# Fused state-space and gated-MLP kernel: later weight loads slot by slot over 128 partitions, and a reordered head

## The chip, the cores and the metric

One NeuronCore of a Trainium2 chip. The metric is the device time of one execution in microseconds; 182.97 is the median of three runs before the change (182.96 to 183.09). Beside it stands one profiled execution, which all views of the trace come from. PE is the matrix engine, DVE the vector engine, ACT the scalar engine, POOL the GpSimd engine, SP the engine whose queue issues most of the loads and stores.

## The reference

```python
def _A_ref(x, ...):                     # state space, P = D = 448 states
    Lam_bar = jnp.exp(dt * Lam)
    B_bar = ((Lam_bar - 1.0) / Lam)[:, None] * Bmat
    Bu = jnp.einsum("bld,pd->blp", x + 0j, B_bar)
    for t in range(L):                  # L = 2048 tokens
        h = Lam_bar[None, :] * h + Bu[:, t, :]
        hs.append(h)
    return 2.0 * jnp.einsum("blp,dp->bld", hseq, Cmat).real + x * Dskip

def _B_ref(x, w_gate, w_up, w_down):    # 448 -> 1792 -> 448
    g = jnp.einsum("bsd,df->bsf", x, w_gate)
    u = jnp.einsum("bsd,df->bsf", x, w_up)
    return jnp.einsum("bsf,fd->bsd", _sigmoid(g) * u, w_down)

xn = _layernorm(x)
out = x + _A_ref(xn, ...) * _silu(_B_ref(xn, ...))
```

All arrays are bfloat16: x is 1 x 2048 x 448, w_gate and w_up are 448 x 1792 each.

## The kernel before

The 2048 tokens are 16 tiles of 128 (x_all, loaded by load_x), taken in 4 chunks of 512. A chunk is normalized and transposed to xnT (feature rows in partitions, tokens along the free side). Its 448 feature rows are 7 slots of 64; xnT holds the slots twice, in partitions 0 to 63 and, rotated, in partitions 64 to 127, so that two matmuls of 64 rows run side by side. The weights wG and wU lie the same way: 7 slots of 64 rows; partitions 0 to 63 hold columns 0 to 895 of w_gate or w_up, partitions 64 to 127 columns 896 to 1791.

For each chunk PE runs 7 pairs of tiles of w_gate ("g" tiles m = 0 to 6) and of w_up ("u"); gu_mm (lines 805 to 809) gives each tile seven steps of two matmuls: step s takes slot s from partitions 0 to 63 and slot s+1 (mod 7) from 64 to 127. ACT takes the tanh of a g tile (gu_evac), DVE multiplies it into the u tile (hF, line 844). Then come the products with B (b_phase; bT and bT6 hold B transposed, bT3 its last rows), the scan on DVE, and in the following chunks the products with C (yout) and w_down (down), the gating and the stores.

Chunk 0 goes g0 to g6, u0 to u6, then b_phase; its head (lines 1099 to 1156) is written out by hand with one order for ACT and DVE (pl.seq): statistics of token tiles 0 to 3 (bn, aggr, root, recip, norm), PE transposes (split for tile 0, first_slots for tiles 1 to 3), copies out of PSUM (ACT, lines 578 and 592), copies within SBUF (DVE, line 599), and the 64-row matmuls of g0 and g1 for one token tile at a time (last_tile, line 814, with slots "a", "b", "c" or 1).

Every operation is given to a planner (class Plan) with a cost, the keys that it reads and writes, and for loads a landing time; solve lays them out and emit issues each engine's instructions in that order. The costs and landing times in the code decide only that order. Waits on the chip come from the data. Loads and stores on SP and ACT share eight completion semaphores in turn, so a load is issued only once the eighth before it has landed.

The loads that matter here: x tiles 0 to 3 and the first 256 columns of wG (load_w0, two queues), then on SP the rest of wG in four loads of 64 partitions (load_w), x tiles 4 and 5, wU's first block, x tiles 6 and 7, the rest of wU; then B by four DMA transposes (b_load), Dskip (dbc), the transposes of chunk 1, w_down (wd), C.

Of the kernel before, what the change touches and what calls it, by code (L numbers as in the profile page):

```python
# [14 lines left out]
ACT = mybir.ActivationFunctionType  # L15
# [3 lines left out]
D = 448  # L19
# [7 lines left out]
TPC = L // P  # L27
NTAB = L + 1
EPS = 1e-5
HEAD_DMA = 19  # L30
TWO_PI = 2.0 * math.pi
PI = math.pi
MAGIC = 12582912.0
# [213 lines left out]
def kernel(  # L247
# [118 lines left out]
    def load_w(eng, k, half, b, r=(), rate=105e3, land=0.0):  # L366
        m0, m1 = BLK[k][b]
        ps = slice(half * H, half * H + H)
        c0 = half * 896
        load(eng, [("w", k, half, m) for m in range(m0, m1)], H * 7 * (m1 - m0) * P * 2,  # L370
             wgt[k][ps, :, m0 * P:m1 * P],
             wsrc[k][:, c0 + m0 * P:c0 + m1 * P].rearrange("(s p) f -> p s f", p=H), cost=0.65, r=r, rate=rate, land=land)

    def load_w0(eng, half, part, r=(), land=0.0):
        ps = slice(half * H, half * H + H)
        s0, c0 = (1 - half if part == "A" else half), half * 896
        n = 4 - s0
        load(eng, [("w", "g", half, m, part) for m in range(2)], H * n * 2 * P * 2, wgt["g"][ps, s0:7:2, 0:2 * P],
             wsrc["g"][:, c0:c0 + 2 * P].rearrange("(s p) f -> p s f", p=H)[:, s0:7:2, :], cost=0.5, r=r, rate=400e3, land=land)

    def wkeys(k, m, part=None):
        if k == "u" or m > 1:
            return [("w", k, 0, m), ("w", k, 1, m)]
        if part == "b":
            return [("w", k, 0, m, "A"), ("w", k, 1, m, "A")]
        return [("w", k, h, m, q) for h in range(2) for q in "AB"]
# [14 lines left out]
    def load_p(eng, k, r=()):  # L401
# [13 lines left out]
    add("POOL", 0.15, lambda: G.memset(ident[:], 0.0), w=["ident"], chain=True)  # L415
    add("POOL", 0.4, lambda: G.affine_select(out=ident[:], in_=ident[:], compare_op=ALU.not_equal, fill=1.0, base=0,
                                             pattern=[[-1, P]], channel_multiplier=1), r=["ident"], w=["ident"], chain=True)
    load_w("SP", "g", 0, 1, rate=400e3, land=8.5)
    load_w("SP", "g", 1, 1, rate=400e3, land=9.5)
    load_w("SP", "g", 0, 2, rate=400e3, land=11.0)  # L420
    load_w("SP", "g", 1, 2, rate=400e3, land=12.4)
    load_x(4, 2, land=13.8)
    add("POOL", 0.1, lambda: G.memset(halfc[:], 0.5), w=["consts"])
    add("POOL", 0.1, lambda: G.memset(negc[:], -1.0), r=["consts"], w=["consts"])
    add("POOL", 0.1, lambda: G.memset(expc[:], math.e), w=["expc"])
# [3 lines left out]
                                    allow_small_or_imprecise_dtypes=True), w=[("wv", 0)])  # L429
    add("POOL", 0.15, lambda: G.memset(flat(g_raw[:, 512:2048], 3, 512)[:, :, D:512], 0.0),  # L430
        w=[("xnw", t) for t in (1, 2, 3)])
    load_w("SP", "u", 0, 0, rate=400e3, land=15.6)
    load_w("SP", "u", 1, 0, rate=400e3, land=16.8)
    load_x(6, 2, land=17.9)
    load_w("SP", "u", 0, 1, rate=400e3, land=19.0)
    load_w("SP", "u", 1, 1, rate=400e3, land=20.1)
    load_w("SP", "u", 0, 2, rate=400e3, land=21.6)
    load_w("SP", "u", 1, 2, rate=400e3, land=23.1)


    def warm_mm(n, w=512):
        def f():
            for _ in range(n):
# [14 lines left out]
    def stats(t):  # L458
        bn(t)
        aggr(t)  # L460
# [19 lines left out]
        ks = lambda k: [(k, t) for t in range(t0, t0 + n)]  # L480
        add("DVE", 0.08, lambda: V.reciprocal(out=rsd[:, t0:t0 + n, :], in_=sdb[:, t0:t0 + n, :]), r=ks("sd"), w=ks("rs"))

    def root(t):
        add("ACT", 0.2, lambda: A.activation(sdb[:, t, :], mvf[:, t, 1:2], ACT.Sqrt, bias=epsc[:]),
            r=[("mv", t), "sqrttab", "epsc"], w=[("sd", t)], lat=0.16)

    def act_mean(t):
        add("ACT", 0.62, lambda: A.activation(junk[:], x_all[:, t, :], ACT.Identity, scale=-1.0 / D, accum_out=nmf[:, t, :]),
# [122 lines left out]
    def xr(c, lo=0, hi=TPC):  # L611
        return [("xnT", c % 3, j, h) for j in range(lo, hi) for h in "ab"]
# [127 lines left out]
        add("POOL", 0.2, lambda: G.tensor_copy(out=sa7[H:P, :], in_=C("n2r")[H:P, 3:4]), r=["n2r"], w=["sa7b"])  # L740

    def b_load():
        for i, m in enumerate((A_B_re, A_B_im)):
            tload([("bT", i)], bT[:, 0:3, i, :], m[:, 0:384], D * 768, land=25.0 + 1.7 * i)
            tload([("bT3", i)], bT[:, 3:4, i, :], m[:, 320:448], D * 256, land=25.7 + 2.0 * i)
            add("POOL", 0.7, lambda i=i: G.tensor_copy(out=bT6[:, 0:3, i * H:i * H + H], in_=bT[:, 0:3, i, 384:448]),
                r=[("bT", i)], w=[("bT6", i)])
            if i == 0:
                add("POOL", 0.45, lambda: G.tensor_copy(out=bT[0:H, 3, 0, :], in_=bT[H:P, 3, 0, :]),
                    r=[("bT3", 0)], w=["bT3l"])  # L750
            for h in range(2):
                add("POOL", 0.25, lambda i=i, h=h: G.tensor_copy(out=bT6[h * H:h * H + H, 3, i * H:i * H + H],
                                                                        in_=bT[H:P, 3, i, 384:448]),
                    r=[("bT3", i)], w=[("bT6", i, h)])

    def c_load():
        for i, m in enumerate((A_C_re, A_C_im)):
# [56 lines left out]
    def last_tile(c, k, steps, j, hs="ba"):  # L814
        x, w_ = xnT[c % 3], wgt[k]
        ts = slice(j * P, j * P + P)
        for h in hs:
            ss = {"a": (0, 2, 4, 6), "b": (1, 3, 5), "c": (0, 2, 4), 1: (6,)}[h]
            for m, a in steps:
                ms = slice(m * P, m * P + P)  # L820

                def f(ms=ms, a=a, ss=ss):
                    for s in ss:
                        go, end = (s == 1, s == 6) if hs[0] == "b" or hs == "a" else (s == 0, s == 5)
                        T.matmul(gu[a][:, 0, ts], lhsT=w_[0:H, s, ms], rhs=x[0:H, SL[s], ts], start=go, stop=end)
# [44 lines left out]
    def b_phase(c, mid=None):  # L870
        x = xnT[c % 3]
        slots = [next_gu() for _ in range(3)]
        a3 = (next_acc(), next_acc())
        bk = [("bT", 0), ("bT", 1), ("bT3", 0), ("bT3", 1), "bT3l"]
        bk6 = [("bT6", 0), ("bT6", 1)] + [("bT6", i, h) for i in range(2) for h in range(2)]
        rs = [(slice(0, H), SL[6]), (slice(H, P), SL[5])]

        def halfrows(pt, start):
# [37 lines left out]
                        r=[("acc", a3[i])] + ([("bus", u, i, 0)] if h else []),  # L916
                        w=[("bus", u) if h == i == 0 else ("bus", u, i, h)])

        add("PE", 0.54, pairs, r=xr(c) + bk + bk6, w=key(3) + key(0) + key(1), name=f"bp{c}")
        for pt in (3, 0, 1):  # L920
            add("PE", (1.29 if pt < 3 else 0.66) + (SW if pt == 3 else 0), lambda pt=pt: fulls(pt, False),
                r=xr(c) + bk + bk6 + key(pt), w=key(pt), name=f"b{c}.{pt}")
# [3 lines left out]
        add("PE", 1.29, lambda: fulls(2, True), r=xr(c) + bk, w=key(2), name=f"b{c}.2")  # L926
        add("PE", 0.22 + SW, lambda: halfrows(2, False), r=xr(c) + bk + key(2), w=key(2), name=f"bp{c}.2")
        evac(2)

    bus_of = {}  # L930
# [127 lines left out]
    def yout(c, j, first=False):  # L1058
        t = c * TPC + j
        g, o, q = gt_of[c, j], next_o(), t % NXD  # L1060
        a = next_acc()
        key, ok, od = ("acc", a), ("o", o, 0), o_t[o][:]
        y = y_mm(c, j, acc[a], key, 0, D, False, first)
        add("DVE", dve1(D), lambda: V.tensor_tensor(out=od, in0=y, in1=xd[q][:], op=ALU.add), r=[key, ("xd", q)], w=[ok])
        add("DVE", dve2(D), lambda: V.tensor_tensor(out=od, in0=od, in1=g_t[g][:], op=ALU.mult), r=[ok, ("gt", g)], w=[ok])
        add("DVE", dve2(D), lambda: V.tensor_tensor(out=od, in0=od, in1=x_all[:, t, :], op=ALU.add), r=[ok, ("x", t)], w=[ok])
        rows = (0, H, P) if c == 2 and j == 3 else (0, P)
        for r0, r1 in zip(rows, rows[1:]):
            store(t, od, 0, D, r0, r1, [ok])

# [39 lines left out]
    aggr(2)  # L1110
    norm(0)
    act_root(1)
    stats(3)
    recip(1, 1)
    norm(1)

    def split(t, keys, banks, eng, between=None):
        pe_transpose(t, [(4, 7, keys[0], banks[0], eng[0]), (0, 4, keys[1], banks[1], eng[1])], between)
# [5 lines left out]
    def between_copies():  # L1124
        copies.append(columns(acc[1][:, 400:412], ("acc", 1)))
        last_tile(0, "g", steps01, 0, "b")
        root(2)
    split(0, ak, ab, ("ACT", "ACT"), between_copies)
    root(3)
    copies[0]()  # L1130
    add("NONE", 0.0, lambda: None, r=["pv0", ("xn", 1)], w=["pv"], lat=0.0)
    first_slots(1, uk[0], ub[0], "ACT")
    last_tile(0, "g", steps01, 0, "a")
    for t in (2, 3):
        recip(t, 1)
        norm(t)
        first_slots(t, ak[t - 2], ab[t - 2], "ACT")
    turns()
    for t in (1, 2, 3):
        shift(t, 1, "DVE")  # L1140
# [3 lines left out]
    scale(1)  # L1144
    silu_table()
    for t in (1, 2, 3):
        last_tile(0, "g", steps01, t, ("c", 1, "b"))
    gu_evac(0, "g", 0, slots0[0])
    gu_evac(0, "g", 1, slots0[1])
    scale(2)  # L1150
# [114 lines left out]
```

## Time and profile before

| | us |
|---|---|
| median of three runs | 182.97 |
| profiled execution, whole | 183.62 |
| its span (first to last instruction) | 181.8 |
| PE busy / DVE busy / ACT busy | 176.3 / 166.4 / 98.1 |
| first transposes on PE | 4.83 |
| g tile 2, first step on PE | 10.40 |
| u tile 0, first step on PE | 17.95 |
| first matmul with B | 28.53 |
| x tiles 4 and 5 read by DVE / tiles 6 and 7 | 13.76 / 18.76 |

Time on PE is dense when the starts follow each other at the pace of the matmuls; busy time alone does not say that, because matmuls overlap. In a timeline row the columns are start, duration, engine, line, operation, output and inputs, and in brackets the idle time before it and what ended it. A window row gives its stretch, the busy time and count of each engine, the granted PE clock, the mean busy share of the 16 DMA engines and GB/s. A queue's row gives its packets, MB and the time of its packets as a share of 16 engines' time.

### The profile page before, as it was taken

To read this page: it belongs to the slowest core of one execution; us is meant where nothing else is said; L and a number is where in the kernel's file an instruction comes from. 1 tells how busy PE (TensorE), PEld (TensorE's weight loads), DVE (VectorE), ACT (ScalarE), POOL (GpSimd) and SP (SyncE) were. 2 spreads that over 40 slices of the span, in tenths; PEclk is the share of its full clock that TensorE was granted. 3 is DMA by queue.
4 is the path that set the end of the run, shared out by engine and by line. 5 is a ranking of instruction groups with operands and counts; after the bars stand their busy time and mean duration, and the time that the engine had idled before them with its cause. 6 is when DMAs were issued, how large, how long until landed. Compare 5 with 4: busy or idle time off the path is not lost.

```text
span 181.8 us, 3610 instructions
## 1 busy us (share of the span) xinstructions
PE 176.3 (97%) x1404; PEld 88.0 (48%) x1411; DVE 166.4 (92%) x294; ACT 98.1 (54%) x162; POOL 37.2 (20%) x93
## 2 busy tenths in 40 slices
PE   8899998999999999999999999999999999999993
PEld 2764444564544444445554444444555444455552
DVE  3866889999989999999999999999999999999772
ACT  4999899958699985364145543348210533411101
POOL 6463556200008797000004100000000000000000
PEclk9999999999999999999999999999999999999999
DMA  5899989999200290000004900001000000002111
GB/s 129 234 216 217 171 159 183 258 251 226 72 0 0 50 140 15 0 4 0 0 2 82 134 14 0 4 0 62 14 4 0 25 27 26 3 0 76 58 54 48
DMA packets 30852, 13.43 MB, mean 74 GB/s; under 512 B 19441, under 2 KB 30834, under 8 KB 30834
## 3 DMA queue, kind: packets, MB, share of 16 engines
q1 hardware_dynamic: 30208, 12.83, 35.0%
q10 hardware_dynamic: 562, 0.36, 0.7%
q8 instruction: 11, 0.18, 0.4%
q14 instruction: 7, 0.06, 0.1%
q0 software_dynamic: 64, 0.00, 0.0%
HBM read 6.77 MB, written 1.84 MB: 47 GB/s over the span
## 4 chain that ended last, share of the span: by engine, by line
PE 81%; DMA 6%; DVE 4%; SPq 4%; ACT 2%; issue 1%; DVEq 0%
PE gu L807 34%; PE gu L1023 15%; PE acc L1042 11%; PE acc L1023 9%; PE gu L895 8%; DMA x_all<-in_A_x_dram 6%; SPq L357 4%; DVE hF L844 2%; PE acc L898 2%; PE gu L881 2%; ACT hT L680 1%; ACT xn L534 1%; DVE bst L450 1%; PE gu L808 1%; DVE spm L687 0%
## 5 line engine op out<-in xcount | busy, mean ns | idle before, releaser
L807 PE MATMUL gu<-xnT,wU 64*128 64x512 bf16 x196 | 45.8, 376 | 0.0
L808 PE MATMUL gu<-xnT,wU 64*128 64x512 bf16 x196 | 45.8, 376 | 0.0
L807 PE MATMUL gu<-xnT,wG 64*128 64x512 bf16 (+1 forms) x189 | 41.3, 360 | 0.0
L808 PE MATMUL gu<-xnT,wG 64*128 64x512 bf16 (+1 forms) x189 | 41.3, 360 | 0.0
L841 ACT ACTIVATE sig<-gu 128x1024 f32<-128x1024 f32 x21 | 21.3, 1019 | 24.7 <-PE gu L808 20.1
L1023 PEld LDWEIGHTS <-hF 128*128 128x128 bf16 x224 | 21.9, 98 | 20.6
L807 PEld LDWEIGHTS <-wU 64*128 64x128 bf16 x196 | 18.4, 94 | 22.9
L807 PEld LDWEIGHTS <-wG 64*128 64x128 bf16 x196 | 18.4, 94 | 19.9
L1023 PE MATMUL gu<-wd,hF 128*128 128x448 bf16 x140 | 28.0, 352 | 0.0
L844 DVE SCALAR_TENSOR_TENSOR hF<-sig,gu 128x1024 bf16<-128x1024 f32 x21 | 25.4, 1210 | 0.7 <-ACT sig L841 0.4
L1042 PE MATMUL acc<-cT,hT 128*128 128x448 bf16 (+2 forms) x119 | 22.9, 337 | 0.0
L962 DVE TENSOR_TENSOR_SCAN wv<-c_r,st,z 128x512 bf16<-128x512 f32 x18 | 22.8, 1273 | 0.0
L1029 ACT ACTIVATE g_t<-gu 128x448 bf16<-128x448 f32 x10 | 5.4, 540 | 27.7 <-PE gu L1023 16.8
L808 PEld LDWEIGHTS <-wU 64*128 64x128 bf16 x196 | 18.4, 94 | 0.0
L808 PEld LDWEIGHTS <-wG 64*128 64x128 bf16 x196 | 18.4, 94 | 0.0
L1023 PE MATMUL acc<-wd,hF 128*128 128x448 bf16 x84 | 16.9, 352 | 0.0
L1042 PEld LDWEIGHTS <-hT 128*128 128x128 bf16 x126 | 11.6, 98 | 9.9 <-issue 0.4
L895 PE MATMUL gu<-xnT,bT 128*128 128x512 bf16 x65 | 15.3, 379 | 0.4
L909 ACT CAST bus<-gu 128x1024 bf16<-128x1024 f32 x12 | 12.0, 1011 | 5.9 <-PE gu L881 5.3
L540 POOL COPY xn<-xn 128x448 bf16<-128x448 bf16 x12 | 7.5, 627 | 28.8 <-ACT xn L534 28.6
L450 DVE BATCH_NORM_STATS2 bst<-x_all 128x6 f32<-128x448 bf16 x11 | 6.4, 616 | 5.8 <-DMA x_all<-in_A_x_dram 5.8
L915 ACT CAST bus<-acc 64x256 bf16<-64x256 f32 (+1 forms) x24 | 8.7, 368 | 4.8 <-PE acc L898 4.4
(161 smaller groups left out, 264.1 us busy)
## 6 DMA issues: line engine op xcount, KB each, us to landing
wd<-in_B_w_down_dram SPq DMA_DIRECT2D x2, 784.0 KB, 6.4
out_dram<-o_t SPq DMA_DIRECT2D x14, 112.0 KB, 1.7
wU<-in_B_w_up_dram SPq DMA_DIRECT2D x4, 224.0 KB, 9.6
x_all<-in_A_x_dram SPq DMA_DIRECT2D x2, 448.0 KB, 5.0
wG<-in_B_w_gate_dram SPq DMA_DIRECT2D x2, 336.0 KB, 6.4
wU<-in_B_w_up_dram SPq DMA_DIRECT2D x2, 336.0 KB, 9.2
wG<-in_B_w_gate_dram SPq DMA_DIRECT2D x2, 224.0 KB, 4.8
x_all<-in_A_x_dram SPq DMA_DIRECT2D x2, 224.0 KB, 7.2
```

The costliest lines, as they stand in the source:

```text
L450: add("DVE", 0.56 if t < TPC else 0.6, lambda: V.bn_stats(out=bst[b][:], in_=x_all[:, t, :]), r=[("x", t)] + ([("xnT", 0, 3, "a")] if 3 < ...
L540: add("POOL", 0.25 if n == H else 0.6, lambda: G.tensor_copy(out=o[:, D:D + n], in_=o[:, 0:n]), r=[("xn", b)], w=[("xnw", b)])
L807: T.matmul(bank[0][:, ts], lhsT=w_[0:H, s, ms], rhs=x[0:H, SL[s], ts], start=(s == 0), stop=(s == 6))
L808: T.matmul(bank[1][:, ts], lhsT=w_[H:P, (s + 1) % 7, ms], rhs=x[H:P, SL[s], ts], start=(s == 0), stop=(s == 6))
L841: add("ACT", act(1024), lambda: A.activation(th, gu[a][:], ACT.Tanh, scale=0.5), r=[("gu", a)], w=[tk])
L844: add("DVE", dve1(1024), lambda: V.scalar_tensor_tensor(out=ho, in0=th, scalar=1.0, in1=gu[a][:], op0=ALU.add, op1=ALU.mult), r=[("gu", a) ...
L895: T.matmul(gu[slots[pt]][:, i, :], lhsT=bT[:, kt, i, pt * P:pt * P + P], rhs=x[:, kt, :], start=(first and kt == 0), stop=(not first and k ...
L909: add("ACT", act(1024), lambda: A.copy(out=bus[u][:], in_=gu[slots[pt]][:]), r=key(pt), w=[("bus", u)])
L915: add("ACT", 0.36, lambda ns=ns, d=d, q=q, l=l, i=i: A.copy(out=bus[u][d, l, ns], in_=acc[a3[i]][q, 0:256]), r=[("acc", a3[i])] + ([("bus" ...
L962: dve(1.194, lambda k=k: V.tensor_tensor_scan(out=wv[:, k, :], data0=rb, data1=z[:, k, :], initial=(st[pt][:, k, :] if c else 0.0), op0=AL ...
L1023: T.matmul(d, lhsT=hF[c % 2][:, m, h, js], rhs=wd[:, ft, :], start=(ft == 0), stop=(ft == FT - 1))
L1042: T.matmul(y, lhsT=hT[c % 2][:, hm, js], rhs=cT[:, cm, c0:c1], start=(i == 0 and not skip_on_pe), stop=(i == 6))
```

## The change

The later weights, that is wG from column 256 and all of wU, are loaded by load_rows: one load for each of the 7 slots, over all 128 partitions. x tiles 4 to 7 are loaded between wG and wU. Of token tile 0, slots 4 to 6 are copied out of PSUM by DVE instead of ACT; one root serves token tiles 2 and 3; the "c" matmuls of tiles 1, 2 and 3 come one tile earlier on PE than before. B's last rows are loaded before the rest of B, and b_phase's first matmuls name only those. The stores of chunk 2 and of chunk 1's last tile go in two halves. Only the first matmul into a bank of g0 and g1 now carries the start flag.

```diff
-HEAD_DMA = 19
+HEAD_DMA = 25
...
+    def load_rows(eng, k, s, m0, m1, land=0.0):
+        src = wsrc[k][s * H:s * H + H, :].rearrange("p (h f) -> h p f", h=2)[:, :, m0 * P:m1 * P]
+        load(eng, ("w", k, "s", s), P * (m1 - m0) * P * 2, wgt[k][:, s, m0 * P:m1 * P], src, cost=0.45, rate=400e3, land=land)
...
         if k == "u" or m > 1:
-            return [("w", k, 0, m), ("w", k, 1, m)]
+            return [("w", k, "s", s) for s in range(7)]
...
-    load_w("SP", "g", 0, 1, rate=400e3, land=8.5)
-    load_w("SP", "g", 1, 1, rate=400e3, land=9.5)
-    load_w("SP", "g", 0, 2, rate=400e3, land=11.0)
-    load_w("SP", "g", 1, 2, rate=400e3, land=12.4)
-    load_x(4, 2, land=13.8)
+    for s in range(7):
+        load_rows("SP", "g", s, 2, 7, land=7.7 + 0.5 * s)
+    load_x(4, 2, land=11.6)
+    load_x(6, 2, land=12.4)
+    for s in range(7):
+        load_rows("SP", "u", s, 0, 7, land=13.2 + 0.7 * s)
...
-    load_w("SP", "u", 0, 0, rate=400e3, land=15.6)
-    load_w("SP", "u", 1, 0, rate=400e3, land=16.8)
-    load_x(6, 2, land=17.9)
-    load_w("SP", "u", 0, 1, rate=400e3, land=19.0)
-    load_w("SP", "u", 1, 1, rate=400e3, land=20.1)
-    load_w("SP", "u", 0, 2, rate=400e3, land=21.6)
-    load_w("SP", "u", 1, 2, rate=400e3, land=23.1)
...
-    def root(t):
-        add("ACT", 0.2, lambda: A.activation(sdb[:, t, :], mvf[:, t, 1:2], ACT.Sqrt, bias=epsc[:]),
-            r=[("mv", t), "sqrttab", "epsc"], w=[("sd", t)], lat=0.16)
+    def root(t, n=1):
+        ts = range(t, t + n)
+        add("ACT", 0.2, lambda: A.activation(sdb[:, t:t + n, :], mvf[:, t:t + n, 1:2], ACT.Sqrt, bias=epsc[:]),
+            r=[("mv", q) for q in ts] + ["sqrttab", "epsc"], w=[("sd", q) for q in ts], lat=0.16)
...
     def b_load():
-        for i, m in enumerate((A_B_re, A_B_im)):
-            tload([("bT", i)], bT[:, 0:3, i, :], m[:, 0:384], D * 768, land=25.0 + 1.7 * i)
-            tload([("bT3", i)], bT[:, 3:4, i, :], m[:, 320:448], D * 256, land=25.7 + 2.0 * i)
...
+        src = (A_B_re, A_B_im)
+        for i in range(2):
+            tload([("bT3", i)], bT[:, 3:4, i, :], src[i][:, 320:448], D * 256, land=19.8 + 1.3 * i)
...
+        for i in range(2):
+            tload([("bT", i)], bT[:, 0:3, i, :], src[i][:, 0:384], D * 768, land=22.6 + 1.7 * i)
...
-                        go, end = (s == 1, s == 6) if hs[0] == "b" or hs == "a" else (s == 0, s == 5)
+                        go, end = (j == 0 and s == 1), (j == 3 and s == 5)
...
-        add("PE", 0.54, pairs, r=xr(c) + bk + bk6, w=key(3) + key(0) + key(1), name=f"bp{c}")
+        add("PE", 0.54, pairs, r=xr(c) + bh + bh6, w=key(3) + key(0) + key(1), name=f"bp{c}")
...
-        rows = (0, H, P) if c == 2 and j == 3 else (0, P)
+        rows = (0, H, P) if c == 2 or (c == 1 and j == 3) else (0, P)
...
-    stats(3)
-    recip(1, 1)
-    norm(1)
...
         last_tile(0, "g", steps01, 0, "b")
-        root(2)
-    split(0, ak, ab, ("ACT", "ACT"), between_copies)
-    root(3)
+        aggr(3)
+        root(2, 2)
+        recip(1, 1)
+        norm(1)
+    bn(3)
+    split(0, ak, ab, ("DVE", "ACT"), between_copies)
...
     last_tile(0, "g", steps01, 0, "a")
+    recip(2, 2)
     for t in (2, 3):
-        recip(t, 1)
         norm(t)
         first_slots(t, ak[t - 2], ab[t - 2], "ACT")
+        if t == 2:
+            last_tile(0, "g", steps01, 1, "c")
...
     for t in (1, 2, 3):
-        last_tile(0, "g", steps01, t, ("c", 1, "b"))
+        if t < 3:
+            last_tile(0, "g", steps01, t + 1, "c")
+        last_tile(0, "g", steps01, t, (1, "b"))
...
-    load("SP", "dbc", P * D * 2, dbc[:], A_Dskip.unsqueeze(0).to_broadcast((P, D)), rate=400e3, land=29.0)
+    load("SP", "dbc", P * D * 2, dbc[:], A_Dskip.unsqueeze(0).to_broadcast((P, D)), rate=400e3, land=26.5)
```

More of the change, by code (lines that the diff above doesn't have):

```diff
@@ L742, in b_load @@
     def b_load():
-        for i, m in enumerate((A_B_re, A_B_im)):
-            tload([("bT", i)], bT[:, 0:3, i, :], m[:, 0:384], D * 768, land=25.0 + 1.7 * i)
-            tload([("bT3", i)], bT[:, 3:4, i, :], m[:, 320:448], D * 256, land=25.7 + 2.0 * i)
-            add("POOL", 0.7, lambda i=i: G.tensor_copy(out=bT6[:, 0:3, i * H:i * H + H], in_=bT[:, 0:3, i, 384:448]),
-                r=[("bT", i)], w=[("bT6", i)])
+        src = (A_B_re, A_B_im)
+        for i in range(2):
+            tload([("bT3", i)], bT[:, 3:4, i, :], src[i][:, 320:448], D * 256, land=19.8 + 1.3 * i)
             if i == 0:
@@ L754, in b_load @@
                     r=[("bT3", i)], w=[("bT6", i, h)])
+        for i in range(2):
+            tload([("bT", i)], bT[:, 0:3, i, :], src[i][:, 0:384], D * 768, land=22.6 + 1.7 * i)
+            add("POOL", 0.7, lambda i=i: G.tensor_copy(out=bT6[:, 0:3, i * H:i * H + H], in_=bT[:, 0:3, i, 384:448]),
+                r=[("bT", i)], w=[("bT6", i)])
     def c_load():
@@ L873, in b_phase @@
         a3 = (next_acc(), next_acc())
-        bk = [("bT", 0), ("bT", 1), ("bT3", 0), ("bT3", 1), "bT3l"]
-        bk6 = [("bT6", 0), ("bT6", 1)] + [("bT6", i, h) for i in range(2) for h in range(2)]
+        bh = [("bT3", 0), ("bT3", 1), "bT3l"]
+        bh6 = [("bT6", i, h) for i in range(2) for h in range(2)]
+        bk = {pt: [("bT", 0), ("bT", 1)] if pt < 3 else [("bT6", 0), ("bT6", 1)] for pt in range(4)}
         rs = [(slice(0, H), SL[6]), (slice(H, P), SL[5])]
@@ L917, in evac @@
                         w=[("bus", u) if h == i == 0 else ("bus", u, i, h)])
-        add("PE", 0.54, pairs, r=xr(c) + bk + bk6, w=key(3) + key(0) + key(1), name=f"bp{c}")
+        add("PE", 0.54, pairs, r=xr(c) + bh + bh6, w=key(3) + key(0) + key(1), name=f"bp{c}")
         for pt in (3, 0, 1):
             add("PE", (1.29 if pt < 3 else 0.66) + (SW if pt == 3 else 0), lambda pt=pt: fulls(pt, False),
-                r=xr(c) + bk + bk6 + key(pt), w=key(pt), name=f"b{c}.{pt}")
+                r=xr(c) + bk[pt] + key(pt), w=key(pt), name=f"b{c}.{pt}")
             evac(pt)
@@ L925, in b_phase @@
             mid([None, *((("gu", a), gu[a][:, 0, 0:D]) for a in slots[:2]), None])
-        add("PE", 1.29, lambda: fulls(2, True), r=xr(c) + bk, w=key(2), name=f"b{c}.2")
-        add("PE", 0.22 + SW, lambda: halfrows(2, False), r=xr(c) + bk + key(2), w=key(2), name=f"bp{c}.2")
+        add("PE", 1.29, lambda: fulls(2, True), r=xr(c) + bk[2], w=key(2), name=f"b{c}.2")
+        add("PE", 0.22 + SW, lambda: halfrows(2, False), r=xr(c) + bh + key(2), w=key(2), name=f"bp{c}.2")
         evac(2)
```

## The prediction

> **What bounds the kernel now.** I read the page first, then the PE timeline, then the chain of waits, then the DMA by stretches.
>
> ```profile
> PE 176.3 (97%) x1404; PEld 88.0 (48%) x1411; DVE 166.4 (92%) x294; ACT 98.1 (54%) x162; POOL 37.2 (20%) x93
> PE 81%; DMA 6%; DVE 4%; SPq 4%; ACT 2%; issue 1%; DVEq 0%
> ```
>
> PE is the bound: 81% of the chain that ended last. The edits add and remove no matmul, so they can only change where PE waits. The timeline has two waits after the warm-up:
>
> ```profile
> 6.16 0.21 PE L825 MATMUL gu<-xnT,wG 64*128 64x128 bf16 x1 [0.48 <-ACT xnT L578]
> 29.32 0.39 PE L881 MATMUL gu<-xnT,bT 64*128 64x512 bf16 x2 [0.41 <-DVE hF L844]
> ```
>
> At 6.16 PE had waited for ACT's first copy out of PSUM. At 29.32 it waited for a bank that DVE freed late: the pair before started at 28.53 and a pair lasts 0.2155 us (below), so 28.75 was due and 0.57 us were lost. The chain of waits says why DVE was late (columns: start, us, what):
>
> ```profile
> 8.53 10.21 DMA x_all<-in_A_x_dram
> ...
> 18.76 1.15 DVE bst L450 x2
> ...
> 28.13 1.14 DVE hF L844
> ```
>
> Tokens 6 and 7 of x land at 18.74 and DVE, which works in order, runs behind from there. Everything else is dense, also the first use of the second weight matrix wU. This is its first tile, seven steps of two 64-row matmuls each:
>
> ```profile
> 17.95 0.38 PE L807 MATMUL gu<-xnT,wU 64*128 64x512 bf16 x1
> ...
> 19.03 0.38 PE L807 MATMUL gu<-xnT,wU 64*128 64x512 bf16 x1
> ```
>
> Five steps in 1.08 us: 0.2155 us each. The step at 19.03 is the sixth; it needs slot 5 in partitions 0 to 63 and slot 6 in 64 to 127. The weights are there in time today.
>
> **The change, part by part.** *Loads.* Ten loads of 64 partitions become fourteen of 128 partitions, one slot each: seven of 640 columns (1280-byte rows, 163,840 bytes) for wG, seven of 896 (1792-byte rows, 229,376 bytes) for wU. The bytes are the same. Two things differ: how many partitions a load writes, and the order of its pattern. load_w walks its source with the 64 rows outermost ("p s f"); load_rows walks it "h p f", the 2 column halves outermost, then 64 rows. How a pattern spreads over the 16 DMA engines is what I ask first.
>
> ```profile
> q10 hardware_dynamic: 562, 0.36, 0.7%
> ```
>
> q10 is ACT's queue: four loads, 0.36 MB in all. Their rows make 1 (Lambda_re, one row) + 128 + 128 (x) + 64 x 4 (wG) = 513 packets. The other 49 are 3 x 16 + 1, which I read as a completion packet from each engine that took part: the loads with 64 or 128 outermost ran on 16 engines, the one with a single outermost row on 1. So an engine gets whole pieces of the outermost loop. With 2 outermost the nearest row is the one with 1, and I take 2 engines, one for each half of the partitions; the other end is 16. I also take them to be the same two for all fourteen loads, as a queue that starts at its first engine would choose.
>
> The price of that, from two stretches (the second is the load of wd alone, 896-byte rows; the first mostly 512-byte rows; columns of the q1 lines: packets, MB, share of 16 engines' time):
>
> ```profile
> q1 hardware_dynamic: 781, 0.38, 74.2%
> ```
>
> ```profile
> q1 hardware_dynamic: 1227, 1.09, 106.9%
> ```
>
> ```profile
> 34.00:37.00 3.00, 3.00 (x49) 2.24 (x48) 2.86 (x5) 2.09 (x4) 0.00 (x0) 1.00 1.07 362
> 10.00:15.00 5.00, 5.00 (x65) 2.51 (x60) 3.42 (x9) 4.97 (x7) 2.27 (x4) 1.00 1.16 220
> ```
>
> From 5 to 7 us: 0.742 x 16 x 2 us / 781 = 30.4 ns a packet; from 34 to 37: 1.069 x 16 x 3 us / 1227 = 41.8 ns. That is 0.0297 ns a byte more, so 53.2 ns for 1280 bytes and 68.4 ns for 1792 (estimates). Each of the two engines moves 64 rows of a load: 3.40 and 4.38 us; seven of each: 23.8 + 30.6 = 54.5 us. Ends: 51.0 us if packets overlap by the 6.9% that the share shows above 100; 60.9 us if an engine keeps the 362/16 = 22.6 GB/s of the wd stretch (81,920 x 7 and 114,688 x 7 bytes an engine). I take 54.5, since the two rows show the growth with size.
>
> The head's last load is issued at 3.07 and lands 3.8 us later (median of its kind on the page), at 6.9; the fourteen follow in their queue's order, with x 4 to 7 between them: 2 loads x 16 rows an engine x 41.8 ns = 1.3 us. Slot 6 of wU then lands at 6.9 + 54.5 + 1.3 = 62.7. The sixth step of wU's first tile cannot start before, against 19.0 now: **+43.7 us**. wG's slot 6 (30.7) stalls PE before, but inside that time.
>
> What waits behind: SP issues in order, so B's four transposes follow. Three of today's take 1.25 to 1.46 us of issue each; from 62.7 four end near 68.3, land near 70.3, and POOL's 2.35 us of bT copies end at 72.7. PE comes to them 0.43 + 6 x 1.51 us after 62.7, plus the next item: 74.0. The transposes of chunk 1 (5.4 us now) end near 74.3 and are needed at 79.7; wd (1.3 us of issue, 6.4 to land) comes at 82 and is needed at 88.1. All hidden, the first by 1.3 us only.
>
> *PE's pace after the wait.* The warm-up's matmuls of 512 columns follow each other at twice the 0.2155 us:
>
> ```profile
> 2.85 0.15 PEld L444 LDWEIGHTS <-const-bfloat16-1.0 128*128 128x128 bf16 x1 [0.28 <-issue]
> ...
> 3.28 0.15 PEld L444 LDWEIGHTS <-const-bfloat16-1.0 128*128 128x128 bf16 x1 [0.28 <-issue]
> ```
>
> That pace, 0.43, lasts the 3.7 us of the warm-up, though the granted clock says 1.00. No row shows what follows an idle stretch later on; bounds 0 and 3.7/2 = **+1.8 us**, and I take the latter, as PE would have done one step in 4.4 us for 27 us.
>
> *x 4 to 7 before wU.* DVE's backlog is gone, its work is done while PE waits: **-0.6 us** (the 0.57 at 29.32).
>
> *Head.* VectorE copies slots 4 to 6 (ACT takes 0.46; DVE's nearest rows are 0.29 for 64x384 within SBUF and 0.61 for 448 fp32 columns out of PSUM), behind it come the aggregate (0.18) and the reciprocal and norm of tile 1, so PE's next transposes, which need that norm (6.38 now), move by -0.16 to +0.2. One root of two columns for two of one takes 0.3 of ACT away but waits for the later aggregate. Moving the first pairs puts two more changes between transposes and 64-row matmuls on PE; such a change costs 0.095 us beyond the pace (7.34 to 7.49 against 0.055): +0.19. All of it, -0.3 to +0.4, ends before 12 us and vanishes in the wait for wG: 0. Without that cover it counts in the first rival.
>
> *B's loads reordered, stores of chunk 2 in halves.* Four more store issues of some 0.6 us on SP's queue, which spends 62.5 us waiting for DVE there: 0, at most 0.6 if the last ones queue.
>
> Sum: 43.7 + 1.8 - 0.6 = 44.9 us on the profiled span of 181.8: 226.7. That execution took 183.62 in all, 0.65 above the median; on the median 182.97 the same 44.9 give **227.9 us**. Own range 221 (51.0 us of loads, no slow pace, an earlier start) to 237 (60.9 us, and 2 us for B's transposes).
>
> [...]
>
> **The rivals.** *All sixteen engines serve the new loads (not slower).* Place: the SP queue from 6.9 us. For it: 64-partition loads run at 220 GB/s and wd's 128-partition ones at 362. Then slot 6 of wG lands at 6.9 + 1.147 MB/362 = 10.1 (needed 10.40 + 5 x 0.2155 = 11.5), x 7 at 11.3 instead of 18.74, slot 6 of wU at 6.9 + 3.212 MB/362 = 15.8 (needed 19.0). Only the 0.57 is won; the head gives -0.3 to +0.4, which I put at 0: 182.4. It decides once the loads run on about twelve engines (3.212 MB in the 12.1 us to 19.0 is 265 GB/s, 11.7 engines at 22.6); below that wU is waited for. Against it: the packets of q10. [...]
>
> *Sixteen engines, but the rate stays at 220.* For it: x loads of 128 partitions between 10 and 15 us did no better. wU's slot 6 lands at 6.9 + 14.6 = 21.5, 2.5 us late; less 0.57: 184.9.
>
> *Two engines for each load, but other ones each time.* Up to eight loads are in flight, so the rates add up; but wG's seventh, issued at 3.86 + 6 x 0.62 = 7.6, needs 3.4 us on its pair and the 1.6 that an x load of 112 KB takes to land (2.3) beside its 16 rows an engine (0.7): 12.6, 1.1 late; less 0.57: 183.5. Nothing shows which engine the single-row load took.
>
> **How the numbers follow.** Two fixed engines 0.72; all sixteen 0.18; rate stays 0.05; changing pairs 0.05. The forecast is the likeliest, 227.9. Its own range alone holds under 0.7, so the range reaches down to the second case: 182.0 to 237. What a measurement here can tell from no change is about 0.2%, 0.4 us: faster 0.16 (most of the second case), same 0.04, slower 0.80.
>
> **What would show it.** Right: the new loads take 3 to 5 us each, one after another; the DMA share in the first 60 us is near 2/16; each load has far fewer than 16 completion packets; PE idles in wG's third tile and in wU's first, released by loads of wU near 63, and not at the pairs of B. Wrong: 300 GB/s and more between 7 and 16 us, PE dense from 8 us on.

## The result, and the profile after

The changed kernel takes 230.18 us (median of 6 runs, 229.06 to 230.54), the kernel before 183.05 (6 runs, 182.96 to 183.35): a ratio of 1.256, 95% interval 1.2535 to 1.2593. The forecast was 227.9. All times and ratios here are of fast runs; one run of all, the profiled one of e9 below (289.83 us at a granted clock of 0.647), was slow and counts nowhere. The profiled execution of the changed kernel took 230.13 us with a span of 228.4, 46.6 us more than the 181.8 of before.

Three lines of its page say where. The first two give the granted PE clock and the busy share of the DMA engines, in tenths, for 40 slices of 5.7 us; the third is SP's queue (packets, MB, share of 16 engines' time).

```profile
PEclk9975559955559999999999999999999999999999
DMA  5111311111999991000820000830001000000221
...
q1 hardware_dynamic: 27452, 12.83, 27.4%
```

From the second slice to the tenth (6 to 57 us) the DMA engines are busy for one tenth, but for the fifth, where x is loaded; two of sixteen would be 0.125. And in two stretches of that time PE's clock falls to half. SP's queue moved the same 12.83 MB in 27452 packets, 2756 fewer than the 30208 of before. That number can be taken apart. The rows of the later weights are 1792 in place of 4480. At 16 completion packets for a load or store over 64 or 128 rows (the reading of q10 in the prediction), the ten old loads took 160 away, and the four additional stores add 64. 30208 - 2688 - 160 + 64 leaves 27424, so the fourteen new loads added 28 packets: two each.

The timeline of PE in the changed kernel, the rows with a wait for weights and those where the pace changes (start, duration, engine, line, and in brackets the idle time before and what ended it):

```profile
14.18 0.60 PE L807 MATMUL gu<-xnT,wG 64*128 64x512 bf16 x1 [2.93 <-DMA wG<-in_B_w_gate_dram]
...
30.87 0.60 PE L807 MATMUL gu<-xnT,wG 64*128 64x512 bf16 x1 [2.62 <-DMA wG<-in_B_w_gate_dram]
...
41.02 0.39 PE L807 MATMUL gu<-xnT,wU 64*128 64x512 bf16 x1 [1.67 <-DMA wU<-in_B_w_up_dram]
45.56 0.61 PE L807 MATMUL gu<-xnT,wU 64*128 64x512 bf16 x1 [4.14 <-DMA wU<-in_B_w_up_dram]
...
59.13 0.60 PE L807 MATMUL gu<-xnT,wU 64*128 64x512 bf16 x1 [3.91 <-DMA wU<-in_B_w_up_dram]
63.64 0.60 PE L807 MATMUL gu<-xnT,wU 64*128 64x512 bf16 x1 [3.91 <-DMA wU<-in_B_w_up_dram]
...
68.31 0.60 PE L807 MATMUL gu<-xnT,wU 64*128 64x512 bf16 x1
...
68.74 0.39 PE L807 MATMUL gu<-xnT,wU 64*128 64x512 bf16 x1
...
77.18 1.03 PE L895 MATMUL gu<-xnT,bT 128*128 128x512 bf16 x4
```

and of the kernel before, the first full matmul of B:

```profile
30.63 1.67 PE L895 MATMUL gu<-xnT,bT 128*128 128x512 bf16 x7
```

Each row with a bracket is one step, released by one slot. wG's slots come 3.34 us apart (14.18 to 30.87 in five), wU's 4.52 (41.02 to 63.64 in five), one after another, without overlap. The step at 63.64 is the sixth of wU's first tile, which started at 19.03 before: +44.61. The twelve pairs from there to 68.74 follow each other at 0.43 us, not 0.2155: 5.10 us for 2.59, +2.51. From 68.74 to the first full matmul of B in the timeline at 77.18 are 8.44 us; before, the same work took 19.03 + 2.59 = 21.62 to 30.63, 9.01: -0.57, the wait for DVE that is gone. (In both traces the record of one full matmul ahead of these is missing, so the difference holds.) Together 46.55, the whole growth of the span; behind it the two kernels take the same time. (Between the medians it is 47.1, since the profiled execution of before was one of its longer ones.)

The half clock stands in the windows of the same trace (columns: stretch, length, busy time and count of PE, PEld, DVE, ACT, POOL, granted clock, DMA share, GB/s):

```profile
45.50:63.60 18.10, 2.43 (x8) 0.42 (x8) 0.00 (x0) 4.59 (x10) 0.00 (x0) 0.50 0.53 58
63.60:69.13 5.53, 5.49 (x28) 1.97 (x30) 2.44 (x2) 0.00 (x0) 4.10 (x15) 0.53 1.09 180
69.20:75.00 5.80, 5.80 (x56) 2.55 (x54) 4.72 (x6) 0.00 (x0) 1.84 (x11) 1.00 1.06 220
```

And SP's queue in the timeline, the issues of wG's and wU's loads and the first transpose behind them:

```profile
2.44 18.63 SPq L357 DMA_DIRECT2D wG<-in_B_w_gate_dram  x9
21.12 4.02 SPq L357 DMA_DIRECT2D x_all<-in_A_x_dram  x2
25.19 26.10 SPq L357 DMA_DIRECT2D wU<-in_B_w_up_dram  x7
51.33 6.58 SPq L398 DMA_TRANSPOSE bT<-in_A_B_re_dram  x1
```

Seven issues of wU take 26.10 us in place of some 0.6 us each: SP itself is held up by the loads. Yet it is through with them at 51.3, 12 us before the last one has landed, and starts on B's transposes there.

### The profile page after: what moved, and what is told of

Same layout as the page of the kernel before. It is cut to its first block, busy times and chain, and to the rows that moved or that the text cites. A ratio compares the mean times of both kernels' runs of the same rounds, so it can differ in the third digit from the quotient of the medians.

```text
span 228.4 us, 3619 instructions
## 1 busy us (share of the span) xinstructions
PE 185.5 (81%) x1404; PEld 89.0 (39%) x1411; DVE 166.1 (73%) x294; ACT 97.6 (43%) x160; POOL 38.4 (17%) x93
## 3 DMA queue, kind: packets, MB, share of 16 engines
q1 hardware_dynamic: 27452, 12.83, 27.4%
HBM read 6.77 MB, written 1.84 MB: 38 GB/s over the span
## 4 chain that ended last, share of the span: by engine, by line
PE 70%; SPq 20%; DMA 7%; issue 1%; DVE 1%; DVEq 0%
PE gu L806 27%; SPq L357 20%; PE gu L1023 12%; PE acc L1042 9%; DMA wU<-in_B_w_up_dram 7%; PE acc L1023 7%; PE gu L895 7%; PE gu L807 6%; PE acc L898 1%; PE gu L881 1%; DVE o_t L1084 0%; DVE o_t L1078 0%; PE acc L884 0%; PE acc L1040 0%; DVEq L1084 0%
## 5 line engine op out<-in xcount | busy, mean ns | idle before, releaser
L807 PE MATMUL gu<-xnT,wU 64*128 64x512 bf16 x196 | 50.1, 396 | 21.5 <-DMA wU<-in_B_w_up_dram 21.5
L807 PE MATMUL gu<-xnT,wG 64*128 64x512 bf16 (+1 forms) x189 | 43.7, 369 | 16.6 <-DMA wG<-in_B_w_gate_dram 16.6
L806 PE MATMUL gu<-xnT,wU 64*128 64x512 bf16 x196 | 50.2, 396 | 0.0
L806 PE MATMUL gu<-xnT,wG 64*128 64x512 bf16 (+1 forms) x189 | 43.9, 368 | 0.2 <-DMA wG<-in_B_w_gate_dram 0.2
L807 PEld LDWEIGHTS <-wU 64*128 64x128 bf16 x196 | 19.0, 97 | 31.2 <-DMA wU<-in_B_w_up_dram 24.3
L843 DVE SCALAR_TENSOR_TENSOR hF<-hF,gu 128x1024 bf16<-128x1024 bf16 x7 | 8.5, 1220 | 30.9 <-issue 27.8
L807 PEld LDWEIGHTS <-wG 64*128 64x128 bf16 x196 | 18.8, 97 | 24.1 <-DMA wG<-in_B_w_gate_dram 19.4
L806 PEld LDWEIGHTS <-wU 64*128 64x128 bf16 x196 | 18.9, 97 | 17.1
L806 PEld LDWEIGHTS <-wG 64*128 64x128 bf16 x196 | 18.8, 97 | 16.3 <-DMA wG<-in_B_w_gate_dram 0.4
L840 ACT ACTIVATE hF<-gu 128x1024 bf16<-128x1024 f32 x6 | 6.0, 1020 | 20.5 <-PE gu L807 20.5
```

The costliest lines, as they stand in the source:

```text
L806: T.matmul(bank[0][:, ts], lhsT=w_[0:H, s, ms], rhs=x[0:H, SL[s], ts], start=(s == 0), stop=(s == 6))
L807: T.matmul(bank[1][:, ts], lhsT=w_[H:P, (s + 1) % 7, ms], rhs=x[H:P, SL[s], ts], start=(s == 0), stop=(s == 6))
L840: add("ACT", act(1024), lambda: A.activation(th, gu[a][:], ACT.Tanh, scale=0.5), r=[("gu", a)], w=[tk])
L843: add("DVE", dve1(1024), lambda: V.scalar_tensor_tensor(out=ho, in0=th, scalar=1.0, in1=gu[a][:], op0=ALU.add, op1=ALU.mult), r=[("gu", a) ...
```

## The experiments

Medians, with the kernel before in the same session; intervals are 95%. Some expectations split the time behind 63.64 into +2.65 and -0.75, cut a pair later than the +2.51 and -0.57 above; the sum is the same within 0.04.

**Which part of the change it is.** Two kernels divide it. e2 is the kernel before with the fourteen loads and the order of x alone (the diff), e3 the changed kernel with these lines turned back.

```diff
-    load_w("SP", "g", 0, 1, rate=400e3, land=8.5)
...
+    for s in range(7):
+        load_rows("SP", "g", s, 2, 7, land=7.7 + 0.5 * s)
+    load_x(4, 2, land=11.6)
+    load_x(6, 2, land=12.4)
+    for s in range(7):
+        load_rows("SP", "u", s, 0, 7, land=13.2 + 0.7 * s)
```

> The kernel before with the loads of the change alone (fourteen loads slot by slot, x 4 to 7 between them); head, stores and the order of B's loads as before. Theory: the loads carry the whole loss: 230.2, within 1.0. Rival (the new head or B's order carry part of it): 228.5 or less, or 231.5 or more.

Measured: 230.11 us (229.51 to 230.7, 4 runs), ratio 1.2556 (1.2523 to 1.259).

> The changed kernel with the loads of the kernel before (blocks of 64 partitions, x 6 and 7 behind wU's first block). What is left of the change is the head, B's order and the stores. Theory: no effect that can be told, 182.6 to 183.4, since PE's next transposes wait for the same norm and two more changes between transposes and 64-row matmuls cost 0.19. Rival (VectorE's copy wins the 0.48 us that PE waited at 6.16): 182.5.

Measured: 183.6 us (183.36 to 183.96, 12 runs) beside 183.23, ratio 1.0017 (1.0007 to 1.0028). The loads carry the whole loss, as expected of e2. The rest costs a little by itself, 0.1 to 0.5 us, somewhat more than was expected of e3. One of the waits for DVE in the head, in the timeline of PE in e3:

```profile
6.02 0.23 PE L830 MATMUL gu<-xnT,wG 64*128 64x128 bf16 x1 [0.17 <-DVE rsd L483]
```

e3's g tile 2 starts at 10.78, 0.38 us later than before. Yet the wait for DVE at B's pairs is absent in this trace too, PE's first step of chunk 1 comes at 34.42 instead of 34.62, and the end lies 3.55 us behind the start of the last matmul instead of 3.31. So the two traces are equally long (181.9 and 181.8), and where the medians lose their 0.3 us is not shown.

**How many engines serve a load.** Three kernels change nothing but the rows that a load reads, and with them the outermost count of its source pattern; so they multiply by other weights than the reference.

```diff
-        src = wsrc[k][s * H:s * H + H, :].rearrange("p (h f) -> h p f", h=2)[:, :, m0 * P:m1 * P]
 # e1: 128 outermost
+        r0 = min(s * H, D - P)
+        src = wsrc[k][r0:r0 + P, m0 * P:m1 * P]
 # e5 and e6: n = 4 and n = 8 outermost
+        src = wsrc[k].rearrange("(b r) f -> b r f", b=n)[:, 0:P // n, m0 * P:m1 * P]
```

> The changed kernel, except that each of its fourteen loads reads 128 consecutive rows of one column half (outermost count 128) in place of 2 column halves of 64 rows (outermost count 2). Same bytes, same row lengths, same partitions; the weights in partitions 64 to 127 are other ones than the reference's. Theory (two engines because the outermost count is 2): the loads run on 16 engines near 362 GB/s, wU's slot 6 lands near 16, before it is needed at 19, and the time is 182.4 (181.8 to 183.2); the SP queue's packets rise to those of 16 completions a load, 27,452 + 14 x 14 = 27,648. Rival (single-slot loads, 128 partitions or long rows are slow in themselves, or fourteen loads hold the queue up): 215 or more.

> The changed kernel, but each of the fourteen loads reads its 128 rows as 4 blocks of 32 rows (rows 112 apart), so the outermost count of its source pattern is 4 and not 2; bytes, packets and destination are the same, the weights are other rows of the same matrix. Theory (a load runs on as many engines as its outermost count): four engines, half the measured 3.3 and 4.5 us a load, so slot 6 of wU lands near 9.0 + 7 x (1.65 + 2.25) = 36.3 us, the sixth step of wU's first tile starts there instead of at 19.0 (+17.3), and with 0 to 2.65 us of slow PE pace and -0.75 the time is 199.8 to 202.4; q1 shows 14 x 2 = 28 packets more than the changed kernel, 27480. Rival (what costs is the jump between two far column halves, whatever the number of engines): as with 128 outermost, 183.4. Rival (any short outermost count falls back to two engines): 230.

> The same with 8 blocks of 16 rows (56 rows apart). Theory: eight engines, 0.83 and 1.13 us a load, slot 6 of wU lands near 9.0 + 13.7 = 22.7 us, the sixth step is 3.6 us later than before; with 0 to 2.65 us of slow pace and -0.75, 186.1 to 188.7; q1 shows 14 x 6 = 84 packets more than the changed kernel, 27536. Both rivals as there: 183.4, or 230.

Measured:

| outermost count | time, us | packets over the changed kernel | sixth step of wU's first tile at |
|---|---|---|---|
| 2 (the change) | 230.18 | 0 | 63.64 |
| 4 (e5) | 202.89 (202.74 to 203.6) | 28 = 14 x 2 | 36.92 |
| 8 (e6) | 188.49 (187.85 to 188.82) | 84 = 14 x 6 | 23.88 |
| 128 (e1) | 183.42 (183.19 to 183.79) | 196 = 14 x 14 | no wait for wU |

The packets, from SP's queue on the page of e5:

```profile
q1 hardware_dynamic: 27480, 12.83, 31.8%
```

and of e6:

```profile
q1 hardware_dynamic: 27536, 12.83, 34.4%
```

Each load gains exactly as many completion packets as it should have engines, and each doubling of the count halves the distance between slots: wU's are 4.52 us apart in the changed kernel, 2.27 in e5, 1.13 in e6. e5 lies 0.5 us over its range, since the sixth step comes at 36.92 and not at 36.3. In e5's timeline:

```profile
34.65 0.61 PE L808 MATMUL gu<-xnT,wU 64*128 64x512 bf16 x1 [1.65 <-DMA wU<-in_B_w_up_dram]
36.92 0.60 PE L808 MATMUL gu<-xnT,wU 64*128 64x512 bf16 x1 [1.67 <-DMA wU<-in_B_w_up_dram]
```

The rivals, a cost of the jump between the column halves (183.4 for both) and a fallback to two engines for any short count (230), are out. e1 also shows that bytes, rows and order are harmless by themselves: with 128 outermost the loads cost nothing. The 182.4 that was expected of e1 was not reached; see the section on the prediction.

**Whether the loads add up in one queue.** e9 loads only wU by slots (the diff), e12 only wG, with six block loads in place of the loop over "u".

```diff
-    for s in range(7):
-        load_rows("SP", "g", s, 2, 7, land=7.7 + 0.5 * s)
+    load_w("SP", "g", 0, 1, rate=400e3, land=8.5)
+    load_w("SP", "g", 1, 1, rate=400e3, land=9.5)
+    load_w("SP", "g", 0, 2, rate=400e3, land=11.0)
+    load_w("SP", "g", 1, 2, rate=400e3, land=12.4)
```

> The changed kernel, with wG loaded by the four blocks of the kernel before (64 rows outermost) and only wU by the seven slot loads. Theory (the two engines serve one load after another, so what counts is the bytes of all slot loads together, and wG's waits are only a part of the same queue): the waits of wG's tiles go, wU's slots start near 12 us and follow each other every 4.5 us, slot 6 lands near 12 + 31.5 = 43.5, the sixth step of wU's first tile is 24.5 us later than before, with 2.65 of slow pace and -0.75 the time is 209.6 (207 to 211). Rival (wG's waits hide behind wU's, so that wU alone costs as much): 227 and more.

Measured: 211.1 us (210.04 to 211.82, 3 runs), ratio 1.1511 (1.1458 to 1.1563): at the upper end of what was expected, and far from the rival's 227. No trace of it is used.

> The changed kernel, with wU loaded by the six blocks of the kernel before (64 rows outermost) and only wG by the seven slot loads: the other half of the run with wU alone, whose ordinary executions took 211.1. Theory (one queue of two engines, whose bytes add up): wG's slot 6 lands at 30.9 as in the changed kernel, 19.4 us after the 11.5 at which the sixth step of wG's third tile could start; with 2.65 of slow pace and -0.75 the time is 204.5, and no wait for wU is left over 2 us, since its blocks have until the fifth tile after that. The two excesses, 21.3 here and 27.9 there, then add up to the 46.9 of the whole change and one slow pace more (49.2 against 49.55). Rival (the wU blocks need the two busy engines too, and wait behind wG's rows): 4 us and more over that, with a wait for wU.

Measured: 205.86 us (205.34 to 206.84, 4 runs), ratio 1.1239 (1.1193 to 1.1284), 1.4 us over the expectation. The waits of PE in e12's timeline:

```profile
27.93 0.60 PE L808 MATMUL gu<-xnT,wG 64*128 64x512 bf16 x1 [2.78 <-DMA wG<-in_B_w_gate_dram]
32.15 0.60 PE L808 MATMUL gu<-xnT,wG 64*128 64x512 bf16 x1 [3.61 <-DMA wG<-in_B_w_gate_dram]
```

No wait for wU follows, so the blocks of wU are not held up by two busy engines; but wG's last slot comes 4.2 us after the one before, not 3.3, and lands 1.3 us later than in the changed kernel. That is the 1.4, and probably the blocks of wU are its cause, since they are what differs in the queue. The excesses, 27.9 (e9) and 22.7 (e12), add up to 50.6; the whole change with one slow pace more makes 47.1 + 2.5 = 49.6. So the stalls at wG and at wU are one after the other in one queue, not one hidden behind the other.

**What the slow pace is.** e7 is the changed kernel with work for PE in the waits of wU's first tile, 90 matmuls of ones into a bank that nobody uses then.

```diff
+        fill = {1: 18, 2: 18, 3: 18, 4: 18, 5: 18}
+        idle = gu[(a + 1) % 3] if (c, k, m) == (0, "u", 0) else None
...
             for s in range(7):
+                if idle is not None and s in fill:
+                    for q in range(fill[s]):
+                        T.matmul(idle[:, q % 2, :], lhsT=ones[:, 0:P], rhs=ones[:, 0:512], start=True, stop=True)
                 T.matmul(bank[0][:, ts], lhsT=w_[0:H, s, ms], rhs=x[0:H, SL[s], ts], start=(s == 0), stop=(s == 6))
```

> The changed kernel, with 18 matmuls of ones x ones into an unused bank put ahead of each of the second to sixth steps of wU's first tile, so that PE works through the waits there (3.9 of each 4.5 us). Theory (after an idle stretch PE runs at half pace for about 5 us, and that is the 2.65 us by which the time exceeds the landing): the twelve pairs after 63.64 follow each other at 0.2155 us and the time falls by 2.65 to 227.5. Rival (the pace of 0.43 comes from the loads or from the code, not from idleness): no change, 230.1. If the added matmuls themselves run at half pace, each group takes 7.8 us instead of 3.9, the last ends about 3 us behind the landing, and the time rises to about 233.

Measured: 227.75 us (226.95 to 228.61, 4 runs), 2.43 less than the changed kernel (the two come from different sessions, between which the kernel before moved by 0.15). The timeline of PE in e7:

```profile
59.50 4.11 PE L810 MATMUL gu<-const-bfloat16-1.0 128*128 128x512 bf16 x18
63.54 0.39 PE L811 MATMUL gu<-xnT,wU 64*128 64x512 bf16 x1
...
63.76 0.38 PE L811 MATMUL gu<-xnT,wU 64*128 64x512 bf16 x1
```

and its windows:

```profile
50.00:60.00 10.00, 9.94 (x45) 4.21 (x46) 0.00 (x0) 0.81 (x3) 0.00 (x0) 1.00 0.83 63
60.00:66.00 6.00, 6.00 (x40) 3.14 (x40) 1.30 (x2) 0.00 (x0) 1.54 (x5) 1.00 0.54 119
```

The slot lands at the same time (63.54), the clock stays at 1.00, and the pairs behind follow each other at 0.22 us. So the slow pace behind 63.64 came from idleness, not from the loads or the code.

**Where the 0.6 us of the earlier x went.** e4 is the kernel before with x tiles 6 and 7 loaded ahead of wU; e8 is the kernel before, unchanged, for a second trace.

```diff
     load_x(4, 2, land=13.8)
+    load_x(6, 2, land=14.9)
...
-    load_x(6, 2, land=17.9)
```

> The kernel before with one load moved: x tiles 6 and 7 ahead of wU's first block. Theory (the 0.57 us at the second pair with B comes from their landing at 18.74): they land near 15, wU's blocks 1 us later but still in time, the wait at 29.3 goes, and the time is 182.4. Rival (another wait takes its place, B's own loads or POOL's copies): 182.8 to 183.2.

Measured: 183.4 us (182.99 to 183.85, 12 runs) beside 183.23, ratio 1.0001 (0.9987 to 1.0015): no gain.

> The kernel before, unchanged, for a second trace. Theory (the 0.57 us wait at 29.32 for DVE is in every run, and the earlier x loads win it but lose it elsewhere): the wait is there again and the profiled time is near 183.2. Rival (that wait is only in the slower ones of the ordinary runs, so the 0.6 us that I took off was never there to win in most runs): without the wait the time is near 183.0, with it near 183.6.

Measured: 183.31 us (183.05 to 183.66, 10 runs), the profiled one 183.59. Neither theory holds: the wait for DVE is not there, and the time is the long one all the same. In its place stands another wait, in the head, behind transposes that run slower than in the first trace (six took 0.51 us there from 4.83), in the timeline of PE in e8:

```profile
5.04 0.82 PE L568 MATMUL acc<-ident,g_t 128*128 128x128 bf16 x6
...
6.76 0.23 PE L826 MATMUL gu<-xnT,wG 64*128 64x128 bf16 x1 [0.30 <-DMA wG<-in_B_w_gate_dram]
...
29.12 0.59 PE L881 MATMUL gu<-xnT,bT 64*128 64x512 bf16 x4
```

The same step in e4's profiled execution:

```profile
6.15 0.21 PE L825 MATMUL gu<-xnT,wG 64*128 64x128 bf16 x1 [0.56 <-ACT xnT L578]
```

In e8 PE is 0.59 us later from there on (B's first pair at 29.12, against 28.53 in the first trace of before): about 0.1 by the slower transposes, the rest by the wait for wG's first columns. DVE has caught up by then, and chunk 1 begins at 34.63 instead of 34.62. In e4's trace there is neither wait: chunk 1 begins at 34.02, and the span is 181.2 instead of 181.8. So in these traces the two waits stand beside each other, and taking away one is worth something only when the other is absent. e1's trace is of the same kind: no wait for DVE, one of 0.28 us for wG at 6.74, B's first pair at 29.31; with the new head chunk 1 begins at 34.82, 0.20 us later than before. Of the two traces of the kernel before one has the wait for wG in the head; e1, e7 and e11 have one too, the other traces not. What makes that load late was not tried; that the fastest runs of before (182.96) are free of both waits is only argued.

**What would have served the layout.** Two kernels keep every byte where the change puts it and give each load 64 rows outermost. e10 cuts each slot into its halves, e11 joins slots into groups.

```diff
 # e10: 28 loads
+        for h in range(2):
+            c0 = h * 896
+            load(eng, ("w", k, "s", s, h), H * (m1 - m0) * P * 2, wgt[k][h * H:h * H + H, s, m0 * P:m1 * P],
+                 wsrc[k][s * H:s * H + H, c0 + m0 * P:c0 + m1 * P], cost=0.45, rate=400e3, land=land)
 # e11: 8 loads, (half, first slot, last slot + 1)
+    GRP = ((0, 0, 3), (1, 0, 4), (0, 3, 7), (1, 4, 7))
...
+        load(eng, ("w", k, "grp", i), H * (s1 - s0) * (m1 - m0) * P * 2, wgt[k][h * H:h * H + H, s0:s1, m0 * P:m1 * P],
+             wsrc[k][s0 * H:s1 * H, c0 + m0 * P:c0 + m1 * P].rearrange("(s p) f -> p s f", p=H), cost=0.5, rate=400e3, land=land)
```

> The changed kernel with each slot load cut into its two column halves, 28 loads of 64 rows (64 outermost) in place of 14 of 128; every byte goes where the change wants it. Theory: all sixteen engines serve each load, the 45 us are gone, and SP's issues set the pace: 30 issues of 0.62 us from 3.86 end at 22.5, slot 6 of wU lands near 24.5, 5.5 us late, 188 us; were the issue of so small a load 0.45 us, 17.4, 19.4 and 183.5. Rival (the slot order itself is what costs, not the two engines): above 200.

Measured: 191.29 us (191.18 to 191.5, 4 runs), ratio 1.0437 (1.0413 to 1.046). The engines are not the limit any more, SP is. Its queue in the timeline of e10, and the window of wU's issues, in which the DMA engines are busy for 0.64:

```profile
13.52 1.10 SPq L357 DMA_DIRECT2D x_all<-in_A_x_dram  x2
14.66 9.88 SPq L357 DMA_DIRECT2D wU<-in_B_w_up_dram  x14
...
13.50:24.60 11.10, 9.50 (x70) 3.64 (x70) 4.76 (x16) 7.45 (x11) 2.61 (x5) 0.85 0.64 182
```

An issue takes 0.60 us (median) and they start 0.64 apart, near the 0.62 expected; but one of wG's took 1.28 and one of wU's 1.70, for a reason not shown, and the last ends at 24.5, not 22.5; the last wait of wU's first tile ends at 26.73, 7.7 us after the 19.03 of before.

> The changed kernel with each weight in four loads, two groups of slots (0 to 2 and 3 to 6; 0 to 3 and 4 to 6) for each half of the partitions: 64 rows outermost, 8 loads in place of 14, rows of 1280 and 1792 bytes in place of the 512 and 768 of the kernel before. Two theories of the 220 GB/s that 64-partition loads showed: if the partitions limit it, wU's last group lands near 6.9 + 14.6 = 21.5, 2.5 us late, 185.3 or so; if the short rows did, the rate is near 360, nothing is late, and the time is that of the kernel with 128 outermost, 183.4.

Measured: 186.03 us (185.91 to 186.13, 4 runs), ratio 1.0147 (1.0121 to 1.0174). The rate decides between the two theories; the windows of e11:

```profile
10.00:15.00 5.00, 3.40 (x51) 1.72 (x47) 1.80 (x4) 4.19 (x5) 1.72 (x3) 1.00 1.11 218
15.00:20.00 5.00, 5.00 (x50) 2.27 (x48) 4.97 (x17) 4.22 (x6) 2.88 (x5) 1.00 1.28 228
```

and of e1, with rows of the same length over 128 partitions:

```profile
10.00:15.00 5.00, 5.00 (x86) 2.94 (x80) 4.64 (x14) 4.97 (x6) 3.22 (x7) 1.00 0.99 326
```

The stretches from 10 to 15 us hold the x loads too. Long rows do not lift the 220 GB/s of 64-partition loads; 128 partitions do, in loads that also take one slot each. The place of the loss was another than expected, though. PE waits first for e11's groups of wG (0.76 and 0.83 us, until 13.45) and is about 2 us late from there. wU's last group, due at 21.5, lands at 21.28, but this late PE waits only a little more for it; the row is that of PE's weight load, and the matmuls come 0.30 us late:

```profile
21.32 0.09 PEld L811 LDWEIGHTS <-wU 64*128 64x128 bf16 x1 [0.63 <-DMA wU<-in_B_w_up_dram]
```

Neither kernel beats the one before, and of the versions tried none did.

## Why the prediction held, and where it did not

*The engines.* Right: the step on which the forecast rested, two engines for an outermost count of 2 read off the 562 packets of ACT's queue, is shown by the 28 packets and by the runs with 4, 8 and 128. A load left 2, 4, 8 and 16 completion packets with these four counts, and 16 with 64 outermost: e10's 28 loads in place of the fourteen bring SP's queue from 27452 packets to 27872, 448 - 28 more.

*The price of a load.* 3.40 and 4.38 us were worked out, 3.34 and 4.52 measured: growing the packet's time with its bytes from two short-row stretches was good to 3%. Part of that is luck: the two measured prices are 52.2 and 70.6 ns a packet, 0.036 ns a byte more and not 0.0297, and the line was 0.06 us too high for wG's loads and 0.14 too low for wU's. The fourteen take 55.0 us instead of 54.5, start at 30.87 - 7 x 3.34 = 7.5 instead of 6.9, and x takes 1.1 of the queue instead of 1.3: 0.9 us late in all, +44.6 for +43.7.

*PE's pace after the wait.* Mis-sized: 1.8 us taken, with 1.8 as the upper bound, and 2.51 in the trace (2.43 by e7). The mechanism was right, but the bound was not one: it took the 3.7 us of the warm-up for the longest slow stretch, and this one lasted 5.1. The reading was off as well: in that trace the slow pace ends at 3.68, 2.9 us after the warm-up's first matmul at 0.77, while in e8, the same kernel, the transposes are still slow at 5.66, 4.9 us after it. One trace could not give a bound. The pace gave 0.7 and the landing 0.9 of what was missing: the sum came to 46.6 on the span, for 44.9.

*x earlier.* The 0.57 us is gone from the trace as said (-0.57). As a gain by itself it does not exist in the medians: e4 lies at 1.0001. The step failed in taking a wait of one trace for a wait of every run; e8 has none, and another in its place.

*The head.* At nothing under the cover of the wait for wG: nothing in the sum speaks against it. Without cover all that is left of the change costs about 0.3 us (e3), within the -0.3 to +0.4; that it is the head which costs it is not shown.

*B's loads.* Right in costing nothing, wrong in why. The four transposes were to be issued from 62.7 and end near 68.3, which left 1.3 us of cover. They were issued from 51.3 and ended at 65.2, since SP went on once the last load was accepted (51.3), not once it had landed (63.6); POOL's last copy ends at 68.0, and PE comes to B at 75.4. The 5.6 us for four left out that the first of before's took 4.95; here they took 13.9, and 5.6 in e10, where the loads were nearly through. With a start at 62.7 the 1.3 us would have been too little for anything much over 5.6.

*The rivals.* Sixteen engines would have given 183.4 (e1), not 182.4. In e1's trace the wait for DVE is gone, but B's first pair comes 0.78 us later than in the first trace of before: of that 0.59 stands in e8 too, without the change, and 0.2 comes with the new head. A rate that stays at 220 is what e11 shows for 64 partitions (218 and 228 GB/s), while 128 partitions moved 326 in e1. Other engines for each load are out: the slots of one weight follow each other without overlap, 3.34 and 4.52 us apart.

## What to carry to other kernels

Before two loads are joined into one over all partitions, look at the outermost count of the joined pattern: here 2 in place of 64 cost 47 us, and the same bytes with 128 outermost cost nothing. The packet count of a queue tells it without a timeline: here a load left 2, 4, 8 or 16 completion packets with 2, 4, 8 or 128 outermost. And a wait seen in one trace is worth its length only if no other wait stands ready to take its place; a second trace of the same kernel is the cheapest test.

## What the runs showed of the hardware beyond that

- PE's granted clock fell to half without any gap over 1.9 us in e5: PE waits 0.9 to 1.9 us there for each slot of wG and works 0.4 to 0.6 between, and the window from 14.5 to 20 us shows 0.56. In e6, with waits of 0.4 to 1.0 us, the granted clock of the profiled execution is 1.00. In e10, with waits of 0.4 to 1.0 us as well (0.42, 0.66, 0.96 and 0.89 before the step at 15.36), the window from 15 to 20 us shows 0.66. So the longest wait alone does not decide; what does was not tried.
- In the changed kernel the first step after 1.67 us of idleness (41.02) still ran at full pace, the next, 4.14 us later, at half; full pace came back after 5.1 us of dense work.
- SP was held up with about three slot loads ahead of it on the two busy engines: the issue of wG's slot 3 lasted from 6.77 to 10.76, and slot 0 landed at 10.87; that of wU's slot 6 lasted from 46.9 to 51.3, and it landed at 63.6, 2.7 loads later. What the limit is counted in, loads or rows, was not tried.
- A load of 64 partitions took SP 0.60 us to issue with one slot (median in e10) and about as long with three or four (e11: the six issues of its row for wG, four of them such loads, took 4.02); an x tile over 128 partitions took 0.40 and 0.42 (the first two in the kernel before). So many small loads were paid for on SP.
